# Sharing the float64-to-float32 conversion of the last layer's weights differently among VectorE, ScalarE and GpSimd, as a pipeline over the experts' steps

## The chip, the cores and the metric

The kernel runs on one core of one Trainium2 chip. The metric is the device time of that core in microseconds (us). Engines are named as in the profile: PE is TensorE (matmuls), DVE is VectorE, ACT is ScalarE, POOL is GpSimd, SP is SyncE, whose queue issues nearly all DMAs here.

## The reference, cut to what matters

Linear attention over 4 batches, 8 heads, 576 rows and 64 columns gives 2304 tokens of 512 numbers. A mixture of 8 experts takes the two best experts of each token (each expert two matrices, 512x1024 and 1024x512, with a relu between). A last layer follows:

```
x = attention(q, k, v, w_phi)                      # 2304 x 512
for e in range(8):                                 # two experts per token, gates from a softmax over the two
    h = np.maximum(x[mask] @ w1[e], 0.0)
    out[mask] += top2_w[mask, k, None] * (h @ w2[e])
h = np.maximum(x @ w_in, 0.0)                      # the last layer: 512 x 2048
out = h * h @ w_out                                # 2048 x 512
```

`w_in` and `w_out` are drawn as `randn(...).astype(np.float32) * (1.0 / np.sqrt(n))`, and the factor makes them float64. No engine of the kernel takes float64, so the kernel itself makes float32 numbers out of their bits. That conversion is the subject here.

## The kernel before, in words

**Stages.** Attention and routing come first; each token's row is scattered to 640 slots per expert. Then come the experts, then the last layer. Matmuls run on pairs of numbers: every float32 operand is split into a high part (`fp32r`, copied on ACT) and the low rest (a subtraction), and three products are added (high x high, high x low, low x high).

**Parts and steps.** The experts' rows are cut into ten parts (`parts`, L135). Part 0 is two of the five 128-row tiles of expert 0 and lies beside the end of attention; part 1 is its other three; parts 2 to 7 are experts 1 to 6 with all five tiles; parts 8 and 9 are two and three tiles of expert 7. Each part has 8 steps f (L1065), one for each 128 of the 1024 hidden columns. A step issues, in this order:

- `e_1(pt, f)`: 12 or 24 matmuls into the PSUM banks M0 and M1 (L191). Five tiles are 640 columns, which take both banks, 320 columns in each. Then ACT makes `hh` (relu and rounding, L201) and DVE makes `hl` (L198) out of each bank. The banks are free for the next step's `e_1` when `hl` is done.
- `e_2(pt, f - 1)`: the second matrix of the step before, 15 matmuls for five tiles. In step 7, transposes of the next part's rows (`x_t`, L172) stand between them; they use the banks Tk, M0 and M1 in turn, and DVE makes their low parts (L84). In step 0, the last three-tile share of the part before comes ahead of `e_1`, two tiles of it behind, and ACT and SP bring its results out (`e_y`, L208 and L209).
- two weight pieces of 128x512 (one in parts 8 and 9): `w_conv`, a copy on ACT (L126) and a subtraction on POOL (L127). SP loads each piece one step ahead (`w_load`, L115, four buffers). In step 4 SP also loads the next part's rows, 1280 KB at once (`x_load`, L159).
- the conversion, below.

Each engine takes its instructions in the order in which the program issues them. An instruction that waits holds up all that stands behind it on its engine or queue.

**The conversion.** `w_in` and `w_out` are cut into 64 tiles of 128x256 numbers. A float64 is two 32-bit words, `low` and `high`. For one tile:

- `wide_load` (L916): SP loads 256 KB into one of two buffers `wide`.
- `wide_a`: four operations on DVE. L927 and L928 build `top` (sign, exponent and the upper 20 bits of the fraction as float32), L929 `exp` (the power of two alone), L930 the low word's upper 23 bits behind that exponent. Then two on POOL: L931 `ok` (the square of the high word read as float32) and L932 `w` (the rest of the fraction as a number, too large by 2^20).
- `wide_b`, in the next step: two on DVE, L938 (`w` times 2^-20 plus `top`) and L939 (zero where `ok` is too small, that is for tiny numbers). Then SP stores 128 KB to `win_d` or `wout_d` (L940).

Work space is `wd`, with two sets of five tiles, so tile m uses what tile m - 2 used, and L932 must wait until the store of m - 2 has read its `w`. In each step the conversion comes last (L1087 to L1097): first `wide_b` of the tiles begun in the step before, then `wide_a` of one or two new ones, each followed by a `wide_load` two tiles ahead. The goal of L1090 spreads the 64 tiles over steps 0 to 6 of parts 2 to 7: 42 steps, about 1.5 tiles a step, and none begun in step 7. Part 8 on has none. The last layer reads `win_d` and `wout_d` from part 7's last step on as ordinary weight pieces.

Of the kernel before, what the change touches and what calls it, by code (L numbers as in the profile page):

```python
# [9 lines left out]
FT = mybir.dt.float32  # L10
FR = mybir.dt.float32r
BF = mybir.dt.bfloat16
I32 = mybir.dt.int32
AF = mybir.ActivationFunctionType
# [6 lines left out]
#: float32's smallest normal number as the upper half of a float64, read as float32  # L21
# [8 lines left out]
def kernel(  # L30
# [100 lines left out]
    # ---- experts: parts of an expert's rows (tiles of the slots j * 128 + p)  # L131
# [93 lines left out]
    # ================= linear attention and routing =================  # L225
    with ExitStack() as actx:
# [67 lines left out]
        # first loads, then the constants  # L294
# [46 lines left out]
        # ---- keys: units of two 128-row tiles; unit 0 of a batch is its tail  # L341
# [95 lines left out]
        # ---- queries: blocks of 512 columns; block 0 of a batch is its tail  # L437
# [125 lines left out]
        # ---- routing of a group of G tiles  # L563
# [100 lines left out]
        def r_4(g):  # L664
# [7 lines left out]
            # a rank past the capacity: a row past all, and the last part of the program  # L672
# [4 lines left out]
            if g == 0:  # L677
                # its tokens among the last expert's first rows, or the last part of the program
# [5 lines left out]
            if g == 1:  # L684
                # the first expert's first rows are not written any more
# [60 lines left out]
        # ---- the pipeline  # L746
# [85 lines left out]
        # the last queries and groups, beside the first expert's first part  # L832
# [61 lines left out]
    # ================= experts and the last layer =================  # L894
    wpb[0] = ctx.enter_context(tc.tile_pool(name="wpb", bufs=1))

    with ExitStack() as ectx:
        xp[0] = ep = ectx.enter_context(tc.tile_pool(name="experts", bufs=1))

        # the last layer's weights come as float64: their bits make the nearest float32  # L900
# [18 lines left out]
        wd = [None]  # L919

        def wide_a(m):
            t = WIDE.pop(m)
            low, high = t[:, :, 0], t[:, :, 1]
            if wd[0] is None:
                wd[0] = ep.tile([128, 2, 5, 256], I32, name="wd", tag="wd", bufs=1)
            ok, top, exp, rest, w = (wd[0][:, m % 2, i] for i in range(5))
            nc.vector.tensor_scalar(rest, high, 3, 0x3FFFFFF8, op0=OP.logical_shift_left, op1=OP.bitwise_and)  # L927
            nc.vector.scalar_tensor_tensor(top, high, -0x40000000, rest, op0=OP.bitwise_and, op1=OP.bitwise_or)  # L928
            nc.vector.tensor_scalar(exp, top, -0x800000, None, op0=OP.bitwise_and)  # L929
            nc.vector.scalar_tensor_tensor(rest, low, 9, exp, op0=OP.logical_shift_right, op1=OP.bitwise_or)  # L930
            nc.gpsimd.tensor_mul(ok.bitcast(FT), high.bitcast(FT), high.bitcast(FT))  # L931
            nc.gpsimd.tensor_sub(w.bitcast(FT), rest.bitcast(FT), exp.bitcast(FT))  # L932
            WIDE[m] = (ok.bitcast(FT), top.bitcast(FT), w.bitcast(FT))

        def wide_b(m):
            (r0, c0), n, _, dst = wide_ap(m)
            ok, top, w = WIDE.pop(m)
# [283 lines left out]
```

## Time and profile before

| | |
|---|---|
| median of 3 runs | 1170.96 us (1170.23 to 1171.25) |
| span of the profiled execution, first to last instruction | 1169.6 us |
| what lies around it, taken as median less span | 1.36 us |
| PE busy | 1113.4 us (95% of the span) |
| DVE busy | 682.4 us (58%) |
| ACT busy | 453.5 us (39%) |
| POOL busy | 439.3 us (38%) |
| mean granted TensorE clock | 0.980 |

The profiled execution has no time listed beside its span; the median less the span stands for what lies around it. The shares are means over stages that differ much: the page's slices show DVE at seven to nine tenths in the stretch where the experts and the conversion are, and at one to four tenths behind it. So the experts' stage, from about 327 to 702 us, must be read by itself. In the fences, a timeline row gives the start, the duration, the engine, the line, the operation and, in brackets, how long its engine was idle before and what ended that.

### The profile page before, as it was taken

What the parts mean: (1) busy time and instruction counts of PE and PEld (TensorE: products, weight loads), DVE (VectorE), ACT (ScalarE), POOL (GpSimd) and SP (SyncE); (2) the same over time, 40 slices, a digit from 0 to 9 for tenths busy, and PEclk for the clock granted to TensorE, in tenths of its full rate; (3) what the DMA queues carried; (4) which work ended last, traced back from release to release, by engine and by line L of the source; (5) the groups of instructions that cost most, each with busy time, mean ns of one, the idle gap of its engine ahead of it and who ended that gap; (6) DMA issues with size and microseconds to landing.
All of it is one profiled execution on the core that took longest, in us unless ns stands there. A gap on an engine that the chain in (4) does not pass through costs nothing.

```text
span 1169.6 us, 17636 instructions
## 1 busy us (share of the span) xinstructions
PE 1113.4 (95%) x6588; PEld 941.7 (81%) x6588; DVE 682.4 (58%) x1311; ACT 453.5 (39%) x897; POOL 439.3 (38%) x438
## 2 busy tenths in 40 slices
PE   7999889989999999999899989999999999999997
PEld 5777767677888988888798978878898888888885
DVE  6778678764178897878898881334243233233222
ACT  5767566732432423232324233443233222232221
POOL 3323353643665565655574754555011010000000
PEclk9999899989999999999999999999999999999999
DMA  5777262424645565555454545442022011000001
GB/s 141 218 194 238 73 190 71 175 108 164 207 148 178 165 199 162 184 172 197 140 192 164 181 145 167 124 148 85 1 73 55 18 37 54 18 10 36 1 1 39
DMA packets 106365, 142.50 MB, mean 122 GB/s; under 512 B 17570, under 2 KB 59682, under 8 KB 105762
## 3 DMA queue, kind: packets, MB, share of 16 engines
q1 hardware_dynamic: 100514, 122.44, 33.2%
q0 software_dynamic: 5760, 18.88, 5.0%
q8 instruction: 54, 0.88, 0.3%
q14 instruction: 37, 0.30, 0.1%
HBM read 92.97 MB, written 48.31 MB: 121 GB/s over the span
## 4 chain that ended last, share of the span: by engine, by line
PE 57%; DVE 18%; issue 9%; DMA 7%; POOL 5%; ACT 1%; another core or an unknown queue 1%; SPq 0%; POOLq 0%; ACTq 0%
PE M L80 23%; PE N L80 10%; PE KV L80 9%; PE P L80 6%; PE Tq L80 5%; DVE wd L939 4%; DVE wd L938 3%; DMA wout_d<-wd 3%; DMA win_d<-wd 2%; DVE wd L928 2%; POOL wd L932 1%; DVE wd L929 1%; DVE wd L930 1%; DVE wd L927 1%; DVE hl L198 1%
## 5 line engine op out<-in xcount | busy, mean ns | idle before, releaser
L1000 DVE TENSOR_TENSOR r<-M,r 128x512 f32<-128x512 f32 (+1 forms) x80 | 51.0, 638 | 245.4 <-ACT h2h L999 245.4
L201 ACT ACTIVATE hh<-M 128x320 fp32r<-128x320 f32 (+2 forms) x128 | 50.8, 436 | 265.8 <-PE M L80 258.6
L996 ACT ACTIVATE r<-M 128x512 f32<-128x512 f32 (+1 forms) x80 | 44.4, 555 | 247.9 <-PE M L80 244.6
L474 POOL PARTITION_ALL_REDUCE qmx<-ps x36 | 70.0, 1945 | 136.6 <-ACT ps L472 132.3
L198 DVE SCALAR_TENSOR_TENSOR hl<-M,hh 128x320 fp32r<-128x320 f32 (+2 forms) x128 | 58.0, 484 | 85.6 <-ACT hh L201 85.6
L938 DVE SCALAR_TENSOR_TENSOR wd<-wd 128x256 f32<-128x256 f32 x64 | 73.1, 1143 | 19.1 <-POOL wd L932 18.6
L961 POOL DMA_INDIRECT yb<-y_d,yrows x18 | 17.7, 981 | 175.8 <-DVE ya L970 173.4
L932 POOL TENSOR_TENSOR wd<-wd 128x256 f32<-128x256 f32 x64 | 47.9, 749 | 88.7 <-DVE wd L930 61.2
L80 PEld LDWEIGHTS N<-kvc,qp 128*128 128x128 f32 x512 | 62.8, 198 | 16.7 <-issue 11.1
L80 PE MATMUL N<-kvc,qp 128*128 128x81 f32 x512 | 67.8, 286 | 8.6 <-issue 3.2
L939 DVE SCALAR_TENSOR_TENSOR wd<-wd 128x256 f32<-128x256 f32 x64 | 73.8, 1153 | 2.2
L1001 DVE TENSOR_TENSOR h2l<-r,h2h 128x512 fp32r<-128x512 f32 (+1 forms) x80 | 57.6, 720 | 7.0
L931 POOL TENSOR_TENSOR wd<-wide 128x256 f32<-128x256 f32 x64 | 49.5, 773 | 0.0
L999 ACT ACTIVATE h2h<-r 128x512 fp32r<-128x512 f32 (+1 forms) x80 | 47.1, 589 | 2.6
L80 PE MATMUL M<-x,w30h 128*128 128x512 f32 (+1 forms) x160 | 45.9, 371 | 0.0
L80 PE MATMUL M<-x,w20h 128*128 128x512 f32 (+1 forms) x160 | 45.7, 370 | 0.0
L80 PE MATMUL M<-x,w10h 128*128 128x512 f32 (+1 forms) x160 | 45.7, 370 | 0.0
L80 PE MATMUL M<-x,w00h 128*128 128x512 f32 (+1 forms) x160 | 45.5, 369 | 0.0
L127 POOL TENSOR_TENSOR w20l<-wstage,w20h 128x512 fp32r<-128x512 f32 x20 | 27.2, 1361 | 43.8 <-ACT w20h L126 28.0
L80 PE MATMUL M<-xth,w10h 128*128 128x320 f32 (+2 forms) x128 | 34.2, 325 | 6.1 <-DVE hl L198 6.1
L739 POOL DMA_INDIRECT xg_d<-x,slots x32 | 31.8, 995 | 21.0 <-DVE slots L700 11.1
L127 POOL TENSOR_TENSOR w30l<-wstage,w30h 128x512 fp32r<-128x512 f32 x20 | 26.7, 1335 | 33.9 <-ACT w30h L126 29.7
(427 smaller groups left out, 3380.7 us busy)
## 6 DMA issues: line engine op xcount, KB each, us to landing
wstage<-in_moe_w_dram SPq DMA_DIRECT2D x128, 256.0 KB
xg_d<-zero SPq DMA_DIRECT2D x8, 1280.0 KB
y_d<-y SPq DMA_DIRECT2D x40, 256.0 KB
xg<-xg_d SPq DMA_DIRECT2D x7, 1280.0 KB
wide<-in_moe_w_in_dram SPq DMA_DIRECT2D x32, 256.0 KB
wide<-in_moe_w_out_dram SPq DMA_DIRECT2D x32, 256.0 KB
kt<-in_k_dram SPq DMA_DIRECT2D x16, 256.0 KB
vt<-in_v_dram SPq DMA_DIRECT2D x16, 256.0 KB
```

The source lines that it names most:

```text
L80: nc.tensor.matmul(o, l, r, start=start, stop=stop, skip_group_check=True)
L127: (nc.gpsimd if n >= 2 else nc.vector).tensor_sub(lo[:, c], src, hi[:, c].bitcast(FT))
L198: nc.vector.scalar_tensor_tensor(hl[:, c0:c1], o, 0.0, hh[:, c0:c1].bitcast(FT), op0=OP.max, op1=OP.subtract)
L201: nc.scalar.activation(hh[:, c[1]:c[2]], c[0], AF.Relu)
L474: nc.gpsimd.partition_all_reduce(mx, ps, 128, bass.bass_isa.ReduceOp.absmax)
L931: nc.gpsimd.tensor_mul(ok.bitcast(FT), high.bitcast(FT), high.bitcast(FT))
L932: nc.gpsimd.tensor_sub(w.bitcast(FT), rest.bitcast(FT), exp.bitcast(FT))
L938: nc.vector.scalar_tensor_tensor(w, w, 2.0 ** -20, top, op0=OP.mult, op1=OP.add)
L939: nc.vector.scalar_tensor_tensor(w, ok, TINY * TINY, w, op0=OP.is_ge, op1=OP.mult)
L999: nc.scalar.activation(hh[:, :n], r[:, :n], AF.Square)
L1000: nc.vector.tensor_mul(r[:, :n], t[:, :n], r[:, :n])
L1001: nc.vector.tensor_sub(hl[:, :n], r[:, :n], hh[:, :n].bitcast(FT))
```

## The change: what it does

The conversion gets other operations on other engines, four work sets in place of two, three load buffers in place of two, and another place for its stores and loads.

- ACT takes two operations per tile, both issued behind the step's `w_conv`: `part` is the upper 16 bits of the low word, read as 16-bit integers and scaled by 2^-36, and `ok` is the square that POOL made before. The lower 16 bits of the low word are no longer used.
- DVE keeps the three operations that make `top` and `exp`. The fourth (L930) goes.
- POOL has one operation per tile, `part` times `exp` (`wide_p`). It is issued in the step after `wide_a`, ahead of that step's `w_conv`.
- `wide_b`, at the end of that step: on DVE, an addition of `top` and `part`, and the same last operation with `ok` as before.
- The store (`wide_store`) and the next loads are issued at the start of the step after `wide_b` (`wide_issue`), ahead of that step's `x_load` and `w_load`. In step 0 they come behind the `e_y` stores of the first three tiles.
- Weights of 2.5 for every step of parts 2 to 7, step 7 included, and 1.0 for those of part 8 spread the 64 tiles: 10 in each of parts 2 to 7 and 4 in part 8, so 1.25 a step in place of 1.5.
- The first three `wide` loads are issued in the first step of part 1, ahead of its `w_load`; before, there were two ahead of the loop.
- The four sets are the ten slots of `wd` and six in three buffers of the tag `ya`, which the last layer uses later. `yb` has three buffers, with `wide`.

```diff
-            t = ep.tile([128, 256, 2], I32, name="wide", tag="wide", bufs=2)
+            t = ep.tile([128, 256, 2], I32, name="wide", tag="wide", bufs=3)
...
-            nc.vector.tensor_scalar(rest, high, 3, 0x3FFFFFF8, op0=OP.logical_shift_left, op1=OP.bitwise_and)
-            nc.vector.scalar_tensor_tensor(top, high, -0x40000000, rest, op0=OP.bitwise_and, op1=OP.bitwise_or)
-            nc.vector.tensor_scalar(exp, top, -0x800000, None, op0=OP.bitwise_and)
-            nc.vector.scalar_tensor_tensor(rest, low, 9, exp, op0=OP.logical_shift_right, op1=OP.bitwise_or)
-            nc.gpsimd.tensor_mul(ok.bitcast(FT), high.bitcast(FT), high.bitcast(FT))
-            nc.gpsimd.tensor_sub(w.bitcast(FT), rest.bitcast(FT), exp.bitcast(FT))
+            ok, top, exp, part = wide_set(m)
+            nc.scalar.activation(part, next16, AF.Copy, scale=2.0 ** -36)
+            nc.scalar.activation(ok, high.bitcast(FT), AF.Square)
+            topi, expi = top.bitcast(I32), exp.bitcast(I32)
+            nc.vector.tensor_scalar(expi, high, 3, 0x3FFFFFF8, op0=OP.logical_shift_left, op1=OP.bitwise_and)
+            nc.vector.scalar_tensor_tensor(topi, high, -0x40000000, expi, op0=OP.bitwise_and, op1=OP.bitwise_or)
+            nc.vector.tensor_scalar(expi, topi, -0x800000, None, op0=OP.bitwise_and)
+
+        def wide_p(m):
+            _, _, exp, part = wide_set(m)
+            nc.gpsimd.tensor_mul(part, part, exp)
...
         def wide_b(m):
+            ok, top, exp, part = wide_set(m)
+            nc.vector.tensor_add(exp, top, part)
+            nc.vector.scalar_tensor_tensor(exp, ok, TINY * TINY, exp, op0=OP.is_ge, op1=OP.mult)
...
-            nc.vector.scalar_tensor_tensor(w, w, 2.0 ** -20, top, op0=OP.mult, op1=OP.add)
-            nc.vector.scalar_tensor_tensor(w, ok, TINY * TINY, w, op0=OP.is_ge, op1=OP.mult)
-            nc.sync.dma_start(dst[r0:r0 + 128, c0:c0 + 256], w)
+            nc.sync.dma_start(dst[r0:r0 + 128, c0:c0 + 256], wide_set(m)[2])
...
+        wweight = [(2.5 if 2 <= pt < NP - 2 else 1.0 if pt == NP - 2 else 0.0) for pt in range(NP)]
...
+        def wide_issue():
+            for m in WS:
+                wide_store(m)
+            WS.clear()
+            while WN[0] < NW and WN[0] - WF[0] < 3:
+                wide_load(WN[0])
+                WA.append(WN[0])
+                WN[0] += 1
...
+        def wide_step(weight):
+            while WP:
+                m = WP.pop(0)
+                wide_b(m)
+                WS.append(m)
+            wdone[0] += weight
+            while WF[0] < min(round(NW * wdone[0] / wtotal), WN[0]):
+                m = WA.pop(0)
+                wide_a(m)
+                WP.append(m)
+                WF[0] += 1
...
                 if f == 0 and pt > 1 and pe != e:
                     e_2(pt - 1, NF - 1, range(p0, p1 - 2))
+                if wide:
+                    wide_issue()
                 if f == 4 and new:
                     x_load(pt + 1)
...
+                if wide:
+                    wide_scale()
                 for p in pieces[pt, f]:
                     w_conv(*p)
                 if wide:
-                    while WB:
-                        wide_b(WB.pop(0))
-                    goal = 64 * (7 * (pt - 2) + min(f + 1, 7)) // 42 if 2 <= pt < NP - 2 else 0
...
+                    wide_step(wweight[pt])
```

More of the change, by code (lines that the diff above doesn't have):

```diff
@@ L13 @@
 I32 = mybir.dt.int32
+U16 = mybir.dt.uint16
 AF = mybir.ActivationFunctionType
@@ L917, in wide_load, with wide_set @@
             WIDE[m] = t
-        wd = [None]
+        WSETS = 4
+        wslots = []
+        def wide_set(m):
+            if not wslots:
+                t = ep.tile([128, 10, 256], FT, name="wd", tag="wd", bufs=1)
+                wslots.extend(t[:, i] for i in range(10))
+                for _ in range(3):
+                    t = ep.tile([128, 2, 256], FT, name="wx", tag="ya", bufs=3)
+                    wslots.extend(t[:, i] for i in range(2))
+            return wslots[m % WSETS * 4:m % WSETS * 4 + 4]
@@ L921, in wide_a @@
         def wide_a(m):
             t = WIDE.pop(m)
[L923 to L933, printed above, removed]
+            high = t[:, :, 1]
+            next16 = t.rearrange("p a b -> p (a b)").bitcast(U16).rearrange("p (a b) -> p a b", b=4)[:, :, 1]
@@ L955, in l_gather @@
                 ya = YA[-1][:, i]
-                yb = ep.tile([128, DM], FT, name="yb", tag="wide", bufs=2)
+                yb = ep.tile([128, DM], FT, name="yb", tag="wide", bufs=3)
             else:
                 ya = ep.tile([128, DM], FT, name="ya", tag="ya", bufs=3)
-                yb = ep.tile([128, DM], FT, name="yb", tag="wide", bufs=2)
+                yb = ep.tile([128, DM], FT, name="yb", tag="wide", bufs=3)
             for c, y in enumerate((ya, yb)):
@@ L1044, with wide_scale @@
         todo = [p for o in order for p in pieces.get(o, [])]
-        WL, NW, WN, WB = [0], [0], [2], []
+        WL = [0]
+        WA, WP, WS, WN, WF = [], [], [], [0], [0]
+        NW = 64
+        wweight = [(2.5 if 2 <= pt < NP - 2 else 1.0 if pt == NP - 2 else 0.0) for pt in range(NP)]
+        wtotal = NF * sum(wweight)
+        wdone = [0.0]
+        def wide_issue():
[6 more added lines that the diff above has]
+                WN[0] += 1
+        def wide_scale():
+            for m in WP:
+                wide_p(m)
+        def wide_step(weight):
[9 more added lines that the diff above has]
+                WF[0] += 1
         def ahead_load(n):
@@ L1056 @@
         ahead_load(2)
-        if wide:
-            wide_load(0)
-            wide_load(1)
         for pt in range(1, NP):
@@ L1087 @@
                 if wide:
-                    while WB:
-                        wide_b(WB.pop(0))
-                    goal = 64 * (7 * (pt - 2) + min(f + 1, 7)) // 42 if 2 <= pt < NP - 2 else 0
-                    while NW[0] < goal:
-                        wide_a(NW[0])
-                        WB.append(NW[0])
-                        NW[0] += 1
-                        if WN[0] < 64:
-                            wide_load(WN[0])
-                            WN[0] += 1
+                    wide_step(wweight[pt])
+                    assert len(WP) + len(WS) <= WSETS
                 if pt == NP - 1 and f in GATHER:
@@ L1101 @@
                     l_sum(0, GATHER.index(f - 1))
+        assert not wide or (WF[0] == NW and not WP and not WS)
         for i in range(R):
```

2 lines of the change are left out of this document (1 added, 1 removed).

## The prediction, made before the changed kernel was run

> **What bounds the kernel now.** I read the page's head first.
>
> ```profile
> span 1169.6 us, 17636 instructions
> ...
> PE 1113.4 (95%) x6588; PEld 941.7 (81%) x6588; DVE 682.4 (58%) x1311; ACT 453.5 (39%) x897; POOL 439.3 (38%) x438
> ```
>
> PE is busy for all but 56 us, and the change touches no matmul. So what the conversion can give is only what PE loses by waiting beside it. The view of PE's waits, from 330 us to the end, names those losses (total, times, longest):
>
> ```profile
> PE M L80 <- DVE hl L198: 11.8, 5, 3.4
> PE M L172 <- DVE hl L198: 5.8, 4, 2.0
> ...
> PE Tq L80 <- ACT hh L201: 0.5, 1, 0.5
> ```
>
> In the experts' stage PE waits almost only for `hl`: 17.6 us in nine waits. The matmuls or transposes that wait need a bank M0 or M1 that DVE has not yet read. The waits cost more than their length. The windows around one of them, a transpose's in step 7 of part 3, show it; the columns are the window, its length, busy time (count) of PE, PEld, DVE, ACT and POOL, the granted clock, the DMA share and GB/s:
>
> ```profile
> 435.00:440.00 5.00, 3.04 (x19) 2.38 (x18) 4.79 (x11) 1.37 (x3) 2.84 (x5) 1.00 0.29 98
> 440.00:445.00 5.00, 5.00 (x22) 4.07 (x22) 2.17 (x4) 1.79 (x3) 0.20 (x1) 0.66 0.48 159
> ```
>
> In the first, PE stands still for 1.96 of 5 us. Behind it the clock falls to 0.66 for some 5 us, another loss of 0.34 x 5 = 1.7 us. Waiting and clock together are best read from the step's rhythm, that is from ACT's `hh` instructions, one per step and bank pair. Here are the first of parts 2, 3, 4 and 5, the last of part 5, the first three of part 6, and the first and last of part 7:
>
> ```profile
> 327.14 0.77 ACT L201 ACTIVATE hh<-M 128x320 fp32r<-128x320 f32 x2 [2.92 <-PE M L80]
> ...
> 389.02 0.77 ACT L201 ACTIVATE hh<-M 128x320 fp32r<-128x320 f32 x2 [2.36 <-PE M L80]
> ...
> 450.99 0.77 ACT L201 ACTIVATE hh<-M 128x320 fp32r<-128x320 f32 x2 [2.36 <-PE M L80]
> ...
> 515.52 0.77 ACT L201 ACTIVATE hh<-M 128x320 fp32r<-128x320 f32 x2 [2.36 <-PE M L80]
> ...
> 568.13 0.77 ACT L201 ACTIVATE hh<-M 128x320 fp32r<-128x320 f32 x2 [10.33 <-PE M L80]
> ...
> 579.42 0.77 ACT L201 ACTIVATE hh<-M 128x320 fp32r<-128x320 f32 x2 [2.36 <-PE M L80]
> ...
> 584.36 0.77 ACT L201 ACTIVATE hh<-M 128x320 fp32r<-128x320 f32 x2 [1.58 <-PE M L80]
> 591.30 0.77 ACT L201 ACTIVATE hh<-M 128x320 fp32r<-128x320 f32 x2 [5.14 <-PE M L80]
> ...
> 639.76 0.77 ACT L201 ACTIVATE hh<-M 128x320 fp32r<-128x320 f32 x2 [2.36 <-PE M L80]
> ...
> 691.06 0.77 ACT L201 ACTIVATE hh<-M 128x320 fp32r<-128x320 f32 x2 [9.85 <-PE M L80]
> ```
>
> No PE wait falls between 568.13 and 591.30, so these rows give the undisturbed steps: 11.29 us from step 7 to the next step 0 (transposes between), 4.94 from step 0 to step 1, and 6.94 for every other. A part without loss is 11.29 + 4.94 + 6 x 6.94 = 57.87 us. Parts 2 to 6 took 61.88, 61.97, 64.53, 63.90 and 60.34, so they lost 4.01, 4.10, 6.66, 6.03 and 2.47. Part 7 took 51.30 up to its last `hh`, where 46.58 was due: 4.72. Together 27.99 us. Behind that lie one transpose wait of 0.96 (0.95 for its twin, below) and the 0.5 for `hh`, whose cause is a results store behind the last conversion stores. All of it comes to 29.5 us.
>
> **Why `hl` is late.** The conversion's operations (min, median, max in ns), and the two weight subtractions of a step on POOL:
>
> ```profile
> L927 DVE TENSOR_SCALAR wd<-wide x64: 278/287/700, 328.4 to 691.2; 128x256 int32<-128x256 int32 x64
> L928 DVE SCALAR_TENSOR_TENSOR wd<-wide,wd x64: 424/426/1452, 328.7 to 691.6; 128x256 int32<-128x256 int32 x64
> L929 DVE TENSOR_SCALAR wd<-wd x64: 293/294/1271, 329.2 to 692.5; 128x256 int32<-128x256 int32 x64
> L930 DVE SCALAR_TENSOR_TENSOR wd<-wide,wd x64: 424/426/718, 329.5 to 693.1; 128x256 int32<-128x256 int32 x64
> L931 POOL TENSOR_TENSOR wd<-wide x64: 611/792/803, 332.4 to 692.1; 128x256 f32<-128x256 f32 x64
> L932 POOL TENSOR_TENSOR wd<-wd x64: 723/739/920, 332.9 to 693.6; 128x256 f32<-128x256 f32 x64
> L938 DVE SCALAR_TENSOR_TENSOR wd<-wd x64: 410/1496/1542, 333.7 to 702.2; 128x256 f32<-128x256 f32 x64
> L939 DVE SCALAR_TENSOR_TENSOR wd<-wd x64: 424/1400/1409, 335.2 to 702.7; 128x256 f32<-128x256 f32 x64
> ```
>
> ```profile
> L127 POOL TENSOR_TENSOR w10l<-wstage,w10h x16: 1286/1297/1517, 355.5 to 751.0; 128x512 fp32r<-128x512 f32 x16
> L127 POOL TENSOR_TENSOR w11l<-wstage,w11h x16: 1286/1478/1485, 357.0 to 755.2; 128x512 fp32r<-128x512 f32 x16
> ```
>
> L938 needs 410 ns, but its median is 1496: about one POOL subtraction more. DVE and POOL stand in each other's way, one instruction waiting for the other's end, so DVE loses in a step at most what POOL is busy. And a chain starts the jam, here in part 4:
>
> ```profile
> 480.07 0.38 SPq L159 DMA_DIRECT2D xg<-xg_d  x1
> ...
> 488.29 0.63 ACT L126 ACTIVATE w10h<-wstage 128x512 fp32r<-128x512 f32 x1 [3.83 <-DMA wstage<-in_moe_w_dram]
> 489.41 0.74 POOL L932 TENSOR_TENSOR wd<-wd 128x256 f32<-128x256 f32 x1 [5.65 <-DMA wout_d<-wd]
> 490.18 1.50 DVE L938 SCALAR_TENSOR_TENSOR wd<-wd 128x256 f32<-128x256 f32 x1 [3.89 <-POOL wd L932]
> 490.64 0.77 ACT L201 ACTIVATE hh<-M 128x320 fp32r<-128x320 f32 x2 [1.07 <-PE M L80]
> ...
> 497.07 0.88 DVE L198 SCALAR_TENSOR_TENSOR hl<-M,hh 128x320 fp32r<-128x320 f32 x2
> 497.62 0.81 PE L80 MATMUL M<-xth,w30h 128*128 128x320 f32 x2 [3.44 <-DVE hl L198]
> ...
> 503.07 0.77 ACT L201 ACTIVATE hh<-M 128x320 fp32r<-128x320 f32 x2 [10.63 <-PE M L80]
> ...
> 505.97 0.66 PE L172 MATMUL M<-ident,xg 128*128 128x128 f32 x4 [0.95 <-DVE hl L198]
> ```
>
> The next part's rows go out at 480.07, the conversion store behind them lands late, POOL waits 5.65 us for its `w`, DVE 3.89 for POOL, and the postponed work pushes `hl` to 497.07, where PE had waited since 494.18.
>
> **The change, part by part.** *DVE.* Now, per tile: 0.287 + 0.426 + 0.294 + 0.426 + 0.410 + 0.424 = 2.27 us without contention; 64 tiles in 42 steps are 1.52 a step, so 3.45, and with `hl` (0.88) 4.33. POOL's share that can stand in the way: 1.30 + 1.48 + 1.52 x (0.79 + 0.74) = 5.11. The worst sum is 9.4 in a step of 6.94. After: L930 goes and the addition replaces L938. The trace has no such addition; its bounds are L938's 0.41 and 1.50, and I take 0.41 because what is above it is POOL's time, counted separately. Per tile 1.84, at 1.25 a step 2.30, with `hl` 3.18. POOL: 2.78 + 1.25 x 0.74 = 3.70. The worst sum is 6.88, just inside 6.94. A step with two tiles exceeds it (every third or so) and the next gives it back.
>
> *Work sets and stores.* L932's successor writes no tile that a store reads; DVE's `exp` does, but the store is that of m - 4, issued at least a step before. The 5.65 us goes, with what followed. What is late next is the weight piece on ACT (3.83): it holds up POOL's subtractions, no longer `wide_b`, whose input is issued ahead of them. Already now that wait did not delay `hh` (450.99 + 4.94 + 5 x 6.94 = 490.63, and it came at 490.64).
>
> *ACT.* Two new operations per tile stand in front of the next `hh`, which PE waits for through `hl`. Nearest rows, with a table load and the squares of the last layer:
>
> ```profile
> L999 ACT ACTIVATE h2h<-r 128x512 fp32r<-128x512 f32 x64 | 40.4, 632 | 2.0
> ...
> L83 ACT ACTIVATE qhl<-qt 128x256 fp32r<-128x256 f32 x32 | 13.2, 411 | 0.0
> ...
> L86 ACT ACT_TABLE_LOAD x1 | 1.3, 1283 | 0.7 <-PEq L1216 0.7
> ```
>
> Same size, SBUF to SBUF: 0.411; a read of 16-bit words at a stride has no row, and the far bound is the 0.63 of twice the elements. I take 0.411: DVE's L927 reads every second word at no visible price. A step is then 0.77 + 2 x 0.63 + 1.25 x 0.82 = 3.06 of 6.94. `hl` is due 494.18 - 490.64 = 3.54 after `hh` starts, and both together take at most 0.77 + 0.88 = 1.65, so `hh` may be 1.9 us late before PE notices. In step 5 with its 3.83 wait and two tiles ACT ends at 488.29 + 2 x 0.63 + 4 x 0.411 = 491.2, some 0.6 late: covered. If that cover were gone, it would cost the lateness and a clock dip, six times.
>
> A rule of the Trainium skill stands against moving work here: ScalarE: Activation LUTs, section What ACT_TABLE_LOAD costs, counts about 2.66 us for every switch to a different set of functions. The trace has one load in the whole program, while squares and relus alternate in the last layer; that makes it an unlikely rival, below.
>
> *Step 7 and part 8.* Step 7 now begins a tile; its DVE work lies behind the transposes' low parts, in 11.29 us. Part 8 gets 4 tiles in 8 steps, with one bank per step in turn and half the weight pieces; I cost it at 0, and at most 1 us for each of the four. The third early load delays a weight piece of part 1 by one 256 KB transfer; part 1 too alternates its banks. Cost 0 to 1 us.
>
> *SP.* Stores waited for DVE on SP's queue before and do so now; what stands behind them are the same weight loads, one step ahead. In step 0 the results' stores now go first, which removes the 0.5.
>
> *The sum.* The span and what lies around it are 1169.6 + 1.36 = 1170.96, the runs' median. Less 29.5 that is 1141.5. I leave 1.5 for a remainder at the tightest place, step 7: PE began to wait for a transpose's bank at 505.97 - 0.95 = 505.02, so the first bank's `hl` must end 1.95 us after `hh` starts (503.07), and half of 1.65 is 0.8: 1.1 are free. In step 6 DVE has two tiles to finish and one to begin, and its worst end, 1.65 + 2 x 0.83 + 1.01 + 2.78 + 0.74 = 7.8 after `hh`, is 0.5 past the time at which the next `hl` could start (6.94 + 0.39). Forecast 1143.0 us.
>
> **The rivals.** *A jam remains in steps 6 and 7 (0.20).* DVE's worst sum, 6.88, is so near to 6.94 that late weight pieces push it over once a part. For it: the jam shown starts behind a 1280 KB load, and these loads stay. Against: the sum was 9.4 and PE still lost only 4.7 a part. Price: part 6 shows what one wait per part costs, 2.47; six times 2.47 on 1141.5 gives 1156.3. Table loads would act likewise (0.02 of the 0.20): two a step are 2 x 1.28 = 2.57 on ACT's 3.06, which still fits into 6.94, but in step 5 with two tiles ACT has 0.77 + 1.26 + 1.64 + 2.57, and with the 3.83 wait 10.1: 3.1 late where 1.9 are free, so a wait of 1.2 and its dip of up to 1.7 in each of six parts: 1141.5 + 17 = 1159. By the page's 2.66 each, two loads bring ACT to 8.4 in every step, and the estimate would be 48 steps x 1.4 = 69 us more.
>
> *No change (0.04).* The four sets help nothing, because the program treats `wd` as one tile and the waits for stores remain, or because the jam comes from late weights. Then the chain at 480 to 498 stays as it is: 1171. Against: L927 writes `wd` and waits for no store, so the sets are told apart already; and the jam's last link is DVE's queue, not ACT.
>
> *Slower: ACT becomes the one that releases late (0.06).* A `wide` tile that lands late holds ACT, and `hh` behind it. It decides when the tile lands over 6.94 + 1.9 - 0.82 = 8.0 us behind the start of its step's `hh`. Each such step costs a wait and a dip, about 2.47 as in part 6; 12 of the 48 steps of parts 2 to 7 would eat the whole gain, one in two gives 1141.5 + 24 x 2.47 = 1200.8. For it: SP issues these loads in order behind stores that wait for DVE. Against: they go out up to three tiles ahead, two steps or 13.9 us.
>
> **How the numbers follow.** The forecast has 0.70, and its own range is 1139.5 to 1148: below, part 7's end may have lost a clock dip too, up to 2 us; above, some waits of the smallest kind. The range is 1139.5 to 1157.5: with the larger part of the jam's 0.20 it leaves out some 0.15. The three runs before spread over 0.09%, so about 0.2% (2.3 us) can be told from no change. The forecast and the jam are both faster by more: 0.90. No change has 0.04, slower 0.06.
>
> **What would show it.** Right: PE's waits for `hl` in the experts' stage near 0 in place of 17.6 us; `hh` of full parts 57.9 us apart; no clock window below 0.95 there; POOL's operation on the conversion no longer waiting for a store; the two DVE operations of `wide_b` still at 1.4 to 1.5 us in the median, since POOL's subtractions stay. Wrong: ACT idle for a `wide` load with `hh` late behind it; waits left in steps 6 and 7; waits for `hl` in part 8, whose steps are short; ACT operations of the conversion far over 0.41 us.

## The result, and the profile after

The changed kernel takes 1142.3 us in the median (four runs, 1141.0 to 1144.33), the kernel before 1171.1 on the same chip (1170.23 to 1171.8). The ratio is 0.9745, with a 95% interval from 0.9719 to 0.9772: faster by 2.5%. The forecast was 1143.0.

The head of the profiled execution's page (1142.34 us) and its row of TensorE's granted clock:

```profile
span 1140.6 us, 17665 instructions
...
PE 1101.5 (97%) x6588; PEld 935.0 (82%) x6588; DVE 642.7 (56%) x1247; ACT 493.8 (43%) x1025; POOL 396.8 (35%) x374
...
PEclk9999999998999999999999999999999999999998
```

The span is 29.0 us shorter, with the same 6588 matmuls. PE is busy 11.9 us less, which is the same work without the stretches at a lower clock: 11.3 of it lie between the first `hh` of part 2 and the last of part 7, where the mean granted clock was 0.98 and is 1.00. The other 17.1 were waiting. The view of PE's waits from 330 us to the end has one row left, and it lies in the last layer; the 17.6 us for `hl` are gone:

```profile
PE Tq L81 <- DVE h2l L1017: 0.7, 1, 0.7
```

ACT's `hh` rows give the rhythm: the first of parts 2 to 7, then the last of part 7 with 320 columns and the first behind it with 256.

```profile
327.13 0.77 ACT L202 ACTIVATE hh<-M 128x320 fp32r<-128x320 f32 x2 [2.92 <-PE M L81]
...
385.00 0.77 ACT L202 ACTIVATE hh<-M 128x320 fp32r<-128x320 f32 x2 [1.72 <-PE M L81]
...
442.87 0.77 ACT L202 ACTIVATE hh<-M 128x320 fp32r<-128x320 f32 x2 [1.72 <-PE M L81]
...
500.74 0.77 ACT L202 ACTIVATE hh<-M 128x320 fp32r<-128x320 f32 x2 [1.72 <-PE M L81]
...
558.61 0.77 ACT L202 ACTIVATE hh<-M 128x320 fp32r<-128x320 f32 x2 [1.72 <-PE M L81]
...
616.49 0.77 ACT L202 ACTIVATE hh<-M 128x320 fp32r<-128x320 f32 x2 [1.72 <-PE M L81]
...
663.07 0.77 ACT L202 ACTIVATE hh<-M 128x320 fp32r<-128x320 f32 x2 [4.49 <-PE M L81]
...
672.51 0.39 ACT L202 ACTIVATE hh<-M 128x256 fp32r<-128x256 f32 x1
```

Every part now takes 57.87 us, which is the part without loss that was read from the kernel before. The windows around the worst place of before, kernel before first, then the changed one (busy time of PE, PEld, DVE, ACT and POOL, then clock, DMA share and GB/s):

```profile
480.00:510.00 30.00, 25.61 (x140) 22.60 (x139) 24.15 (x41) 6.99 (x14) 16.01 (x17) 0.94 0.58 189
```

```profile
480.00:510.00 30.00, 30.00 (x177) 27.14 (x177) 23.20 (x39) 15.47 (x34) 14.86 (x13) 1.00 0.56 179
```

DVE is about as busy as before, POOL hardly less, and PE is never idle. The windows hold different steps, so they alone don't tell whether the amount of work or what stands behind what made the difference; the experiments do. The changed kernel's conversion (min, median, max in ns; a part of the tiles, the others write `wx`):

```profile
L939 ACT ACTIVATE wd<-wide x48: 418/432/439, 330.5 to 687.6; 128x256 f32<-128x256 f32 x48
L941 DVE TENSOR_SCALAR wd<-wide x32: 278/289/1387, 328.4 to 681.8; 128x256 int32<-128x256 int32 x32
...
L938 ACT ACTIVATE wd<-wide x32: 421/432/443, 330.2 to 678.9; 128x256 f32<-128x256 uint16 x32
L947 POOL TENSOR_TENSOR wd<-wd x32: 733/742/747, 332.4 to 683.0; 128x256 f32<-128x256 f32 x32
L951 DVE TENSOR_TENSOR wd<-wd x32: 412/416/1535, 333.4 to 683.8; 128x256 f32<-128x256 f32 x32
L952 DVE SCALAR_TENSOR_TENSOR wd<-wd x32: 424/1399/1406, 333.8 to 685.3; 128x256 f32<-128x256 f32 x32
```

The addition's median is its undisturbed length; a blocked one takes up to 1535 ns. In POOL's waits between 320 and 720 us no store is left. What its conversion operation waits for is DVE's `exp` (here for the tiles in `wd`; those in `wx` add as much again):

```profile
POOL wd L947 <- DVE wd L943: 31.7, 26, 1.9
```

### The profile page after: what moved, and what is told of

The parts are those of the page before. It is cut to its first block, busy times and chain, and to the rows that moved or that the text cites. A ratio compares the mean times of both kernels' runs of the same rounds, so it can differ in the third digit from the quotient of the medians.

```text
span 1140.6 us, 17665 instructions
## 1 busy us (share of the span) xinstructions
PE 1101.5 (97%) x6588; PEld 935.0 (82%) x6588; DVE 642.7 (56%) x1247; ACT 493.8 (43%) x1025; POOL 396.8 (35%) x374
## 4 chain that ended last, share of the span: by engine, by line
PE 86%; DVE 6%; DMA 2%; issue 2%; ACT 1%; another core or an unknown queue 1%; POOL 1%; SPq 0%; POOLq 0%
PE M L81 38%; PE N L81 16%; PE KV L81 12%; PE P L81 9%; PE Tq L81 8%; DVE qhl L85 1%; PE Tk L81 1%; PE Tq L461 1%; PE M L173 1%; DMA wstage<-in_moe_w_dram 1%; DVE kmx L374 1%; PE Tk L995 1%; PE Tk L173 1%; PE Tk L356 1%
## 5 line engine op out<-in xcount | busy, mean ns | idle before, releaser
L977 POOL DMA_INDIRECT ya<-y_d,yrows x18 | 17.9, 997 | 187.2 <-PE Tk L995 112.5
L81 PEld LDWEIGHTS N<-kvc,qp 128*128 128x128 f32 x512 | 62.1, 197 | 17.5 <-issue 11.9
L740 POOL DMA_INDIRECT xg_d<-x,slots x32 | 31.9, 997 | 21.7 <-DVE slots L701 11.8
L85 DVE TENSOR_TENSOR qhl<-qt,qhl 128x256 fp32r<-128x256 f32 x32 | 37.0, 1156 | 0.4 <-ACT qhl L84 0.4
L128 POOL TENSOR_TENSOR w10l<-wstage,w10h 128x512 fp32r<-128x512 f32 x16 | 22.3, 1394 | 40.6 <-ACT w10h L127 36.8
L947 POOL TENSOR_TENSOR wd<-wd 128x256 f32<-128x256 f32 x32 | 23.7, 741 | 36.0 <-DVE wd L943 31.7
L947 POOL TENSOR_TENSOR wx<-wx 128x256 f32<-128x256 f32 x32 | 23.7, 740 | 35.1 <-DVE wx L943 31.6
L952 DVE SCALAR_TENSOR_TENSOR wd<-wd 128x256 f32<-128x256 f32 x32 | 35.1, 1096 | 1.1
```

Of the source, the lines that this page charges most:

```text
L81: nc.tensor.matmul(o, l, r, start=start, stop=stop, skip_group_check=True)
L85: nc.vector.tensor_sub(lo, src, hi.bitcast(FT))
L128: (nc.gpsimd if n >= 2 else nc.vector).tensor_sub(lo[:, c], src, hi[:, c].bitcast(FT))
L947: nc.gpsimd.tensor_mul(part, part, exp)
L952: nc.vector.scalar_tensor_tensor(exp, ok, TINY * TINY, exp, op0=OP.is_ge, op1=OP.mult)
```

## The experiments

The theory: PE lost its time through a chain of waits, which begins where POOL's subtraction must wait for the store that still reads its `w`; what removes this wait brings the gain. Its rivals: the amount of work on DVE and POOL decides, whatever waits for what; or weights that arrive late behind the next part's rows; or the order of stores and loads on SP's queue. The letters in the quoted expectations stand for theories as these texts describe them.

The experiments ran on other chips, whose runs of the kernel before took 1164.0 us (first four experiments), 1162.0 (next four), 1162.6 (next three, on the same chip as those four) and 1172.4 (the last); there the first `hh` of part 2 comes up to some 10 us earlier. So I compare ratios to the kernel before on the same chip, and the rhythm: "lost" is the time from the first `hh` of part 2 to that of part 7, less 5 x 57.87 us. It is 23.3 us in the kernel before and 0.0 in the changed one.

**Four `w` and nothing else.** The kernel before with four tiles for `w`, so that the store of m - 2 is no longer in the way.

```diff
-                wd[0] = ep.tile([128, 2, 5, 256], I32, name="wd", tag="wd", bufs=1)
-            ok, top, exp, rest, w = (wd[0][:, m % 2, i] for i in range(5))
+                wd[0] = ep.tile([128, 12, 256], I32, name="wd", tag="wd", bufs=1)
+            ok, top, exp, rest, w = (wd[0][:, i] for i in [m % 2 * 4, m % 2 * 4 + 1, m % 2 * 4 + 2, m % 2 * 4 + 3, 8 + m % 4])
```

> The kernel before, with four tiles w in turn in place of two, so that POOL's L932 writes what the store of tile m - 4 has read; nothing else is changed. Theory A (a chain: SP is late because its loads stand behind DVE, the next part's rows go out late, the store behind them lands late, POOL waits for it with w, DVE for POOL, hl is late): POOL's waits for stores (25.8 us in six) go, and with them most of the 17.6 us that PE waits for hl: 1143 to 1152 us. Theory B (DVE and POOL together simply have more work than a step has time, 9.4 us at worst in 6.94): the waits for hl stay, 1165 to 1171 us.

Measured: 1145.1 us, ratio 0.9827 (0.9799 to 0.9855). No POOL wait for a store is left, and 7.4 us are lost in place of 23.3. PE's waits and, in the second fence, ACT's:

```profile
PE M L172 <- DVE hl L198: 8.3, 5, 2.8
```

```profile
ACT w30h L126 <- DMA wstage<-in_moe_w_dram: 8.8, 3, 3.8
ACT w10h L126 <- DMA wstage<-in_moe_w_dram: 7.7, 3, 3.4
```

The waits of the matmuls for `hl` (11.8 us before) are gone although every operation and the spread are the old ones, and although weights still come late. What stays are the transposes' waits in step 7. So without the store wait some two thirds of the loss go. Step 7 still loses; a kernel below with the same four `w` and fewer tiles a step doesn't, so that there it is the amount of work left at the end of a part.

**The new spread alone.** 1.25 tiles a step with step 7 and part 8, in the kernel before.

```diff
-                    goal = 64 * (7 * (pt - 2) + min(f + 1, 7)) // 42 if 2 <= pt < NP - 2 else 0
+                    goal = 10 * (pt - 2) + 10 * (f + 1) // 8 if 2 <= pt < NP - 2 else 60 + (f + 1) // 2 if pt == NP - 2 else 0
```

> The kernel before, with the 64 tiles spread as in the changed kernel: 10 in each of parts 2 to 7, step 7 included, and 4 in part 8, that is 1.25 a step in place of 1.52; same operations, two work sets, same queues' order. Theory A: fewer steps with two tiles, but the store of tile m - 2 is still waited for behind the 1280 KB load: PE's waits for hl fall by a third to a half, 1155 to 1165 us. Theory B: the work per step falls by 18% and the waits for hl nearly vanish: 1143 to 1150 us.

Measured: 1160.3 us, ratio 0.997 (0.9952 to 0.9989); 17.0 us are lost. POOL's waits for a store became more, 36.4 us in eleven where the same view of the kernel before has 25.8 in six:

```profile
POOL wd L932 <- DMA win_d<-wd: 25.2, 7, 6.3
...
POOL wd L932 <- DMA wout_d<-wd: 11.2, 4, 5.0
```

In sum this spread is worth almost nothing, but the rhythm shows two things that cancel. From step 6 to the next step 0, where the kernel before lost 21.9 us, only 3.0 are lost, although POOL still waits 4.5 to 6.3 us for a store in step 5 of every part. From step 0 to step 3, where the kernel before lost nothing, 14.0 are lost. ACT's waits for a `y` buffer show this new loss; the same row of the kernel before has 6.1 us:

```profile
ACT y L208 <- DMA y_d<-y: 34.8, 6, 7.6
```

So less work per step does take away most of what the store wait cost, and something else eats it; the experiment with four `w` and this spread, below, shows what. This goal isn't quite the spread of the changed kernel either: it begins two tiles in steps 3 and 7 of a part, the changed kernel in steps 2 and 5.

**Rows one step earlier.** In the kernel before, the next part's 1280 KB of rows go out in step 3, behind the weight loads.

```diff
-                if f == 4 and new:
-                    x_load(pt + 1)
...
+                if f == 3 and new:
+                    x_load(pt + 1)
```

> The kernel before, with the next part's rows (1280 KB) issued in step 3, behind its weight loads and ahead of its conversion stores and loads, in place of the start of step 4; this puts them some 7 us earlier. Theory A: the weight pieces of step 5 are no longer late (ACT's 3.83 us wait goes), the store is out of the way of the rows; PE's waits for hl fall by half or more: 1145 to 1158 us. Theory B: no change, 1168 to 1172 us.

Measured: 1164.3 us, ratio 1.0012 (0.9994 to 1.003); 23.9 us are lost. PE's waits, then POOL's:

```profile
PE M L80 <- DVE hl L198: 12.4, 10, 3.7
PE M L172 <- DVE hl L198: 5.7, 4, 2.5
```

```profile
POOL wd L932 <- DMA wout_d<-wd: 18.1, 4, 5.8
...
POOL wd L932 <- DMA win_d<-wd: 7.9, 2, 4.1
```

ACT's long waits for `w10h` and `w30h` (7.7 us each in the kernel before) are down to 1.4 at most for any piece, and nothing is gained. Late weights are not the cause. The store wait stayed: a store stands behind the rows in step 3 too. And the chain moved with the rows. All six of POOL's waits for a store now lie in step 4, where five of six lay in step 5, and 15.5 us are lost from step 5 to step 6, where it was 0.3; from step 6 to step 7 it is 2.7, where it was 14.8.

**The new operations alone.** Two sets, the old places and the old spread.

```diff
+            nc.scalar.activation(part, next16, AF.Copy, scale=2.0 ** -36)
+            nc.scalar.activation(ok.bitcast(FT), high.bitcast(FT), AF.Square)
...
-            nc.vector.scalar_tensor_tensor(rest, low, 9, exp, op0=OP.logical_shift_right, op1=OP.bitwise_or)
-            nc.gpsimd.tensor_mul(ok.bitcast(FT), high.bitcast(FT), high.bitcast(FT))
-            nc.gpsimd.tensor_sub(w.bitcast(FT), rest.bitcast(FT), exp.bitcast(FT))
+            nc.gpsimd.tensor_mul(part, part, exp.bitcast(FT))
...
-            nc.vector.scalar_tensor_tensor(w, w, 2.0 ** -20, top, op0=OP.mult, op1=OP.add)
+            nc.vector.tensor_add(w, top, w)
```

> The kernel before, with the new operations alone: ACT makes part and ok, DVE three operations and then the addition and the last one, POOL one multiplication; two work sets, old places of stores and loads, 1.52 tiles a step. Here ACT's part writes the tile that the store of m - 2 reads, so ACT inherits POOL's wait. Theory A: ACT waits up to 5 us for a store in steps 5 or 6 with hh behind it; the gain is small or none, 1160 to 1175 us. Theory B: DVE and POOL have less work and the waits for hl go: 1143 to 1152 us.

Measured: 1139.3 us, ratio 0.9785 (0.9757 to 0.9813); 3.9 us are lost. ACT's waits, then PE's:

```profile
ACT wd L930 <- DMA wout_d<-wd: 55.3, 12, 7.9
...
ACT wd L930 <- DMA win_d<-wd: 45.6, 12, 6.6
```

```profile
PE M L173 <- DVE hl L199: 2.7, 3, 1.6
PE M L81 <- DVE hl L199: 1.1, 2, 0.9
```

This went against the theory as I had put it. The wait for the store did not go; it moved to ACT, which now writes `w` first, and is four times as long in sum (100.9 us). PE hardly sees it. A wait for a store is therefore not harmful as such. In the kernel before it hurt, where POOL was the one that waited, with DVE queued behind POOL and `hl` behind DVE, and both were full. Here both have less work, and there is room to recover.

**The changed kernel on the same chip** as the three that follow it; nothing is edited.

> The changed kernel as it is, on the same chip as the next three, to compare with them. Both theories: no wait for hl in the experts' stage; 2.2 to 2.8% below the kernel before.

Measured: 1134.5 us, ratio 0.9753 (0.9727 to 0.978), parts of 57.87 us.

**The pipeline with the old operations.** Places, sets and spread of the changed kernel; DVE has its four operations and the old last two again, POOL its square and its subtraction.

```diff
-            nc.scalar.activation(part, next16, AF.Copy, scale=2.0 ** -36)
-            nc.scalar.activation(ok, high.bitcast(FT), AF.Square)
...
+            nc.vector.scalar_tensor_tensor(parti, low, 9, expi, op0=OP.logical_shift_right, op1=OP.bitwise_or)
+            nc.gpsimd.tensor_mul(ok, high.bitcast(FT), high.bitcast(FT))
...
-            nc.gpsimd.tensor_mul(part, part, exp)
+            nc.gpsimd.tensor_sub(part, part, exp)
...
-            nc.vector.tensor_add(exp, top, part)
+            nc.vector.scalar_tensor_tensor(exp, part, 2.0 ** -20, top, op0=OP.mult, op1=OP.add)
```

> The changed kernel with the old operations: four on DVE and the square on POOL in wide_a, the subtraction on POOL where the multiplication stood, two on DVE in wide_b; four sets, the new spread and the new place of stores and loads stay, ACT does nothing for the conversion. Theory C (the wait for a store is the disturbance, and the free time of DVE and POOL decides whether hl feels it; taking away either is enough): no store is waited for, the worst sum of DVE and POOL is 8.4 us a step, PE's waits for hl stay under 5 us: within 0 to 8 us of the changed kernel. Theory B (the worst sum against 6.94 us decides): 15 to 25 us above the changed kernel.

Measured: 1136.1 us, ratio 0.9767 (0.9741 to 0.9794), parts of 57.93 us, 0.25 lost. A window of 60 us:

```profile
330.00:390.00 60.00, 60.00 (x344) 54.38 (x344) 52.86 (x85) 21.76 (x46) 38.00 (x38) 1.00 0.55 182
```

DVE is busy for 52.86 us (88%), more than the 48.44 in the same window of the kernel before, and PE doesn't wait at all. The old operations fit if nothing stops them.

**The new operations with four `w`.** Old places, old spread. The operations are edited as in the new operations alone; the lines below are what comes on top.

```diff
-                wd[0] = ep.tile([128, 2, 5, 256], I32, name="wd", tag="wd", bufs=1)
-            ok, top, exp, rest, w = (wd[0][:, m % 2, i] for i in range(5))
+                wd[0] = ep.tile([128, 12, 256], I32, name="wd", tag="wd", bufs=1)
+            ok, top, exp, rest, w = (wd[0][:, i] for i in [m % 2 * 4, m % 2 * 4 + 1, m % 2 * 4 + 2, m % 2 * 4 + 3, 8 + m % 4])
```

> The kernel before with the new operations and four tiles w in turn; old spread over 42 steps, old places of stores and loads. Theory C: no wait for a store is left and DVE and POOL have 7.6 us at worst: all of the gain, within 2 us of the changed kernel, so spread and order add nothing. Its rival (theory D: the remainder in step 7 needs the new spread): waits of transposes for hl stay and it is 4 to 10 us above the changed kernel.

Measured: 1134.2 us, ratio 0.9757 (0.9731 to 0.9782); 0.3 lost. That is all of the gain, without a new spread or a new place for the stores.

**ACT's operations three times.** In the changed kernel both operations are issued three times, with the same result each time.

```diff
-            nc.scalar.activation(part, next16, AF.Copy, scale=2.0 ** -36)
-            nc.scalar.activation(ok, high.bitcast(FT), AF.Square)
+            for _ in range(3):
+                nc.scalar.activation(part, next16, AF.Copy, scale=2.0 ** -36)
+                nc.scalar.activation(ok, high.bitcast(FT), AF.Square)
```

> The changed kernel with ACT's two operations of each tile done three times (the same results written again), 2.6 us of ACT a tile in place of 0.86. By the prediction's slack (ACT has 6.94 us a step and 1.9 us beyond it before PE notices): 2.03 + 1.25 x 2.6 = 5.3 us a step, 7.2 in a step with two tiles: no change, within 2 us of the changed kernel. By the rival that hh behind them is late at once: up to 48 steps x 2.2 us = 100 us more.

Measured: 1133.4 us, ratio 0.9749 (0.9722 to 0.9775), parts of 57.87 us.

```profile
330.00:390.00 60.00, 60.00 (x343) 54.34 (x342) 46.40 (x75) 41.51 (x109) 31.72 (x27) 1.00 0.57 188
```

ACT goes from 27.5 to 41.5 us of 60, and nothing moves. The prediction's rival for "slower" was a `wide` tile that lands late and holds ACT. ACT waits for no `wide` load in the changed kernel, and in the one with the new operations and four `w`, where it does wait up to 2.6 us for one, only 0.3 us are lost.

**Four `w` and the new spread together**, the first two experiments' edits in one kernel.

```diff
-                wd[0] = ep.tile([128, 2, 5, 256], I32, name="wd", tag="wd", bufs=1)
+                wd[0] = ep.tile([128, 12, 256], I32, name="wd", tag="wd", bufs=1)
...
-                    goal = 64 * (7 * (pt - 2) + min(f + 1, 7)) // 42 if 2 <= pt < NP - 2 else 0
+                    goal = 10 * (pt - 2) + 10 * (f + 1) // 8 if 2 <= pt < NP - 2 else 60 + (f + 1) // 2 if pt == NP - 2 else 0
```

> The kernel before with four tiles w in turn and the new spread (1.25 tiles a step, step 7 included), old operations, old places of stores and loads. Theory C: without waits for stores, the waits of transposes that four w alone left in step 7 come from the two tiles that step 6 finished or began; with less work in step 6 they go: ratio to the kernel before 0.975 to 0.979. Rival (theory E: it was the new place of stores and loads that removed them): they stay, 0.982 to 0.986 as with four w alone.

Measured: 1158.2 us, ratio 0.9965 (0.9946 to 0.9984): much worse than with four `w` alone. Of the 13.6 us lost, all lie between step 0 and step 1, where a part takes up to 8.72 us in place of 4.94 (net 2.24 in one part and 3.77 in each of three); the other steps run undisturbed, step 7 among them. The timeline shows why; the lines of SP are issues of DMAs:

```profile
434.53 0.61 ACT L208 ACTIVATE y<-P 128x512 f32<-128x512 f32 x1
...
436.28 0.33 SPq L940 DMA_DIRECT2D win_d<-wd  x1
...
438.19 2.51 SPq L916 DMA_DIRECT2D wide<-in_moe_w_in_dram  x2
...
440.76 0.81 PE L80 MATMUL M<-xth,w20h 128*128 128x320 f32 x2 [1.77 <-DVE hl L198]
440.79 1.40 SPq L209 DMA_DIRECT2D y_d<-y  x3
...
444.39 0.60 ACT L208 ACTIVATE y<-N 128x512 f32<-128x512 f32 x1 [5.45 <-DMA y_d<-y]
```

In step 7 one tile is now finished and, with this goal, two are begun. The store of the one and the two loads behind it wait on SP for DVE, ahead of the results' stores in step 0. The first three `y` are ready by 435.1, but their stores go out at 440.79; ACT needs the buffers for the next `y`, stands still for 5.45 us, and `hh` stands behind it. On DVE the second tile's operations (438.04 to 440.30) stand ahead of `hl`, for which PE waits 1.77 us. The changed kernel issues the results' stores first and begins one tile in step 7, and ACT waits 0.25 us there:

```profile
382.34 1.31 SPq L210 DMA_DIRECT2D y_d<-y  x3
...
383.79 1.66 SPq L956 DMA_DIRECT2D wout_d<-wd  x1
...
386.70 0.60 ACT L209 ACTIVATE y<-N 128x512 f32<-128x512 f32 x1 [0.25 <-DMA y_d<-y]
```

So the two edits do not add up. Neither expected ratio came: the transposes' waits went, as theory C had it, but a loss that neither theory named took their place. Of the rivals named at the start, the order on SP's queue is at work here; the last experiment changes it alone.

**Three sets.** The changed kernel with `WSETS = 3`.

```diff
-        WSETS = 4
+        WSETS = 3
```

> The changed kernel with three work sets in place of four: DVE's exp of tile m now waits for the store of tile m - 3, which went out at the start of the same or the step before. It brings the wait for a store back, and onto DVE itself, behind whose instructions hl stands. Theory C: DVE waits for stores behind the 1280 KB loads (a few us in steps 4 and 5 of each part), hl is late there, but with 6.9 us of work at worst it catches up: PE's waits for hl 2 to 10 us, ratio 0.977 to 0.985. Theory B (only the sum of work decides): ratio as the changed kernel, 0.973 to 0.977.

Measured: 1133.1 us, ratio 0.975 (0.9721 to 0.9778), 0.3 lost. DVE waits for no store with three sets either. So it shows that the fourth isn't needed. It was to bring the store wait back and didn't, so it decides nothing between the theories.

**DVE's work doubled.** In the changed kernel, all five DVE operations of a tile are done twice, with the same result.

```diff
+            for _ in range(2):
+                nc.vector.tensor_scalar(expi, high, 3, 0x3FFFFFF8, op0=OP.logical_shift_left, op1=OP.bitwise_and)
+                nc.vector.scalar_tensor_tensor(topi, high, -0x40000000, expi, op0=OP.bitwise_and, op1=OP.bitwise_or)
+                nc.vector.tensor_scalar(expi, topi, -0x800000, None, op0=OP.bitwise_and)
...
+            for _ in range(2):
+                nc.vector.tensor_add(exp, top, part)
+                nc.vector.scalar_tensor_tensor(exp, ok, TINY * TINY, exp, op0=OP.is_ge, op1=OP.mult)
```

> The changed kernel with DVE's five operations of each tile done twice (the same results written again): 3.7 us of DVE a tile without contention in place of 1.84, with hl 5.5 a step, and at worst 5.5 + 3.7 = 9.2 us with POOL in the way, as much as in the kernel before; still no wait for a store. Theory C: hl is hardly late, 0 to 8 us above the changed kernel, ratio 0.974 to 0.982. Theory B: as much loss as in the kernel before, ratio 0.99 to 1.01.

Measured: 1203.4 us, ratio 1.035 (1.032 to 1.038); 48.8 us lost. PE's waits, then a window:

```profile
PE M L81 <- DVE hl L199: 28.7, 21, 2.0
PE Tq L81 <- DVE hl L199: 7.6, 4, 2.6
PE M L173 <- DVE hl L199: 6.8, 6, 2.4
```

```profile
450.00:510.00 60.00, 52.11 (x285) 45.24 (x284) 56.75 (x114) 21.45 (x52) 27.09 (x24) 1.00 0.50 162
```

Here no store is waited for, and PE loses more than in the kernel before, and more than either theory gave. So the rival, the amount of work, decides once DVE's work exceeds the time: 56.75 us of 60, with parts of 65 to 70 us. The limit lies between this kernel and the pipeline with the old operations: that one's DVE is busy 52.86 / 60 x 57.93 = 51.0 us of a part, this one's 56.75 / 60 x 69.58 = 65.8 us in part 4, over the 57.87 that a part has.

**The pipeline with old operations, its stores and loads issued ahead of the results' stores** in step 0, so as in the kernel with four `w` and the new spread.

```diff
-                if f == 0 and pt > 1 and pe != e:
-                    e_2(pt - 1, NF - 1, range(p0, p1 - 2))
                 if wide:
                     wide_issue()
+                if f == 0 and pt > 1 and pe != e:
+                    e_2(pt - 1, NF - 1, range(p0, p1 - 2))
```

> The pipeline with the old operations (e6), with one thing moved: the stores and loads of the conversion are issued ahead of the results' stores of step 0, as in the kernel before, in place of behind them. Theory F (four w with the new spread lost at every part's first step because SP, waiting there for DVE's tile of step 7, holds back the results' stores; ACT then waits for a y buffer with hh behind it): ACT's waits for y are 20 us or more, PE loses 2 to 4 us a part at step 0, and the ratio to the kernel before is 0.985 to 0.998 in place of 0.977. Rival (the place of the POOL subtraction, or the third load buffer, made the difference): the ratio stays at 0.975 to 0.980.

Measured: 1154.5 us, ratio 0.9845 (0.9815 to 0.9875), where the same kernel with the results first had 0.9767 (0.9741 to 0.9794). ACT's waits:

```profile
ACT y L209 <- DMA y_d<-y: 21.2, 6, 5.1
```

From part 3 on, every part takes 58.74 to 59.06 us, about 1 more than with the results first (I had expected 2 to 4; but here, unlike with four `w` and the new spread, step 7 begins one tile, not two). More goes at the change to part 8: between 630 and 690 us PE is busy for 56.82 us, and for 57.24 in the next 60, where the kernel with the results first has 58.11 and 59.38. So the order of two issues on SP is worth about a third of the gain; this order is all that differs, though the two ratios come from two chips.

## Why the prediction was right, point by point

**What PE loses.** 29.5 us were read from PE's waits, the clock behind them and the rhythm; the span gave up 29.0. Of it, 28.0 came by the last `hh` of part 7, as the rhythm had it, and every part went to the undisturbed length; 1.0 came behind, where 1.5 were counted. A dip of the clock did not follow every wait: behind the 1.96 us wait in step 7 of part 3 the granted clock was about 0.5 for three us, and 3.75 us were lost; behind the 1.97 us wait in step 7 of part 6 it stayed at 1.00, and 2.18 were lost.

**The chain behind it.** Its last links are right: four `w` alone take the matmuls' waits away. Its first link, the rows ahead of the store, is right too: the waits moved with the rows, though one step earlier gains nothing while some store still stands behind them. But the chain isn't the whole of it. The new operations leave the wait in place, on another engine, and still bring 2.15 of the 2.5%. The new spread leaves it on POOL, and the loss behind it mostly goes. The kernel before needed both: a wait on POOL, and a DVE and POOL so full that the postponed work reached `hl`. Taking the wait away is worth 15.9 us there (23.3 lost against 7.4), 3.4 with the new spread (17.0 against 13.6) and 3.6 with the new operations (3.9 against 0.3). Take either away, and most is gained; the gains don't add, since they are the same 29 us. The prediction counted on both without saying which was enough, and the changed kernel takes away both at once, so its being right doesn't tell them apart. Why ACT's waits of up to 7.9 us cost PE so little is only argued: a `hh` may be 1.9 us late by the prediction's own count, and DVE and POOL have more room.

**The worst sum on DVE.** "6.88, just inside 6.94" made it look tight. It is a bound that the steps did not reach in the mean. From the groups of the six DVE lines, DVE spends 266.5 us on 64 tiles in the kernel before (4.16 each, 2.27 without contention), 224.0 in the changed one (3.50, and 1.84 without). It suffers 1.90 of the 5.11 / 1.52 = 3.36 us per tile that POOL is busy, and 1.66 of 3.70 / 1.25 = 2.96: 56% both times, and 46 to 61% in the other runs. In the pipeline with the old operations DVE spends 273.8 us, 4.28 a tile, so 0.88 + 1.25 x 4.28 = 6.2 us a step, and it indeed loses almost nothing, though its worst sum is 8.4 (1.25 x (2.27 + 1.53) + 2.78 + 0.88). Two tiles begin in two of eight steps, not in every third.

**The addition.** Costed at 0.41 between 0.41 and 1.50, it measured 0.416 in the median and 0.794 in the mean (tiles in `wd`). The view of what would show it said that both operations of `wide_b` would stay at 1.4 to 1.5: half wrong. Only L952 did, and L941, the same operation as L927 before, rose from 427 ns in the mean to 721. The contention moved to other instructions; its amount fell only from 1.90 to 1.66 us a tile.

**ACT.** Costed at 0.411 an operation, measured 0.432, for the 16-bit read as for the square. The cover was ample, as three times the operations show. Table loads were an unlikely rival, and the trace settles it: one in the whole program, as before.

```profile
L87 ACT ACT_TABLE_LOAD x1 | 1.3, 1283 | 0.7 <-PEq L1257 0.7
```

The Trainium skill (ScalarE: Activation LUTs, What ACT_TABLE_LOAD costs) counts about 2.66 us for a switch to a different set of functions. By that rule the two operations aren't a switch here; its load itself shows at 1.283 us, and what it counts beyond that no run here shows.

**What is late next.** The prediction named the weight piece on ACT (3.83 us in the kernel before). It isn't late any more, and I hadn't seen why. The rows' issue on SP in step 4 of part 4, with the step's `hh`, before and after:

```profile
476.76 0.77 ACT L201 ACTIVATE hh<-M 128x320 fp32r<-128x320 f32 x2 [5.14 <-PE M L80]
477.17 2.80 SPq L916 DMA_DIRECT2D wide<-in_moe_w_out_dram  x2
480.07 0.38 SPq L159 DMA_DIRECT2D xg<-xg_d  x1
```

```profile
467.44 0.33 SPq L917 DMA_DIRECT2D wide<-in_moe_w_out_dram  x1
467.89 0.37 SPq L160 DMA_DIRECT2D xg<-xg_d  x1
...
468.63 0.77 ACT L202 ACTIVATE hh<-M 128x320 fp32r<-128x320 f32 x2 [4.49 <-PE M L81]
```

Before, the rows went out 3.31 us after `hh`, behind `wide` loads that took SP 2.80 us; now 0.74 before it. Rows and the weights behind them go out some 4 us earlier in the step. It was covered in any case, as the experiment with the rows shows.

**The results' stores first in step 0.** Costed at 0.5 us removed. Measured in the pipeline it is some 0.8% of the time, because a spread that works in step 7 would have put six waits there. Right that it was put in, mis-sized as to what it prevents. **The remainder** of 1.5 us left for steps 6 and 7 was not there: 1141.5 without it, against 1142.34 for the profiled run and 1142.3 in the median, so step 7 and part 8 cost within 1 us of their 0. That the forecast came within 0.7 us is partly luck: the remainder that wasn't there stood in for a span that gave up 0.5 less than counted and for 1.74 us around it in the profiled run, where 1.36 was taken.

**Left open.** No experiment brought the store wait back into the changed kernel; three sets were not few enough. The changed kernel's own spread, with one tile begun in step 7, was not run by itself. No kernel of the study beats the changed one by more than the intervals: with the new operations and four `w`, with three sets and with ACT's operations three times the ratio is 0.9749 to 0.9757, its own 0.9753 on the same chip.

## What to carry to other kernels

When an engine that issues in order waits for a store, look at who is queued behind it: the wait cost some 16 us on POOL with a full DVE behind, and 3 to 4 where DVE had less work a step or where ACT was the one that waited. A gain that two parts of a change each bring mostly alone is one gain; a spread that evens out work can undo it by putting a store on the queue ahead of another store that somebody needs. And a sum of two engines that block each other is a worst case: measure what share of it is really suffered before calling it tight.

## What the runs showed of the hardware that was not expected

- DVE suffered about half of the time that POOL was busy, 46 to 61% over the runs, not all of it. An instruction mostly takes one of two lengths: of the changed kernel's 64 additions 43 take 0.4 us and 21 take 1.5, with none between; of L952 20 take 0.4 and 44 take 1.4. The Trainium skill (SBUF — State Buffer, SBUF: two separate sides) has DVE and GpSimd share a port pair as an exclusive lock held for a whole instruction; the two lengths agree with that.
- ACT reads every fourth 16-bit word as fast as every second 32-bit word: 432 ns for 128x256 in both.
